# A relu² attention and a relu² feed-forward in one kernel: score visits of three tiles in spare PSUM banks, g sums ahead of squares, and one store per 128 tokens

## Chip, cores and metric

The kernel runs on one core of one Trainium2 chip. The metric is the device time of one execution in microseconds; the median over several executions is compared. The engines are named as the profile names them: PE is TensorE's matmuls, PEld its weight loads, DVE VectorE, ACT ScalarE, POOL GpSimd and SP SyncE.

## The reference, cut to what matters

Attention without softmax over 8 batches, 12 heads, 448 tokens and 64 elements per head, followed by a feed-forward layer from 768 to 2,048 and back.

```python
scores = matmul(q, k.transpose(0, 1, 3, 2)) / sqrt(64)
attn = maximum(scores, 0.0) ** 2 / 448
x = matmul(attn, v)                      # 8 x 12 x 448 x 64
x = x.transpose(0, 2, 1, 3).reshape(3584, 768)
h = x @ w_in                             # 3584 x 2048
g = maximum(h, 0.0) ** 2
out = g @ w_out                          # 3584 x 768, float32
```

## The kernel before, in words

**Tokens.** The 448 tokens of a batch are numbered `p * 7 + j`, with `p` from 0 to 63 and `j` from 0 to 6. A *row* of 128 output tokens is written `(pr, tb)`: pair of batches `pr` (0 to 3) and block `tb` (0 to 6). Its partitions 0 to 63 hold the tokens of one `j` and its partitions 64 to 127 those of the next. In six blocks of seven both `j` belong to one batch; in block 3 the second `j` is 0 of the pair's other batch.

**Attention.** A *unit* is four heads of one batch, three units to a batch, 24 in all. A unit has seven *score tiles*, one per `j`. `score(t)` computes one: four 64x64 matmuls of 448 columns that run side by side on the four quarters of the array, into a `slot` of two PSUM banks (two slots, `s_p`), and one ACT instruction (line 266) that takes the relu of 128x896 out of PSUM into an `at` tile. DVE squares it in place (line 369). When all seven tiles of a unit are there, `av_unit` multiplies them with v (28 matmuls, line 317), also into a slot, and ACT copies the result to `xt` (line 323).

**Feed-forward.** Batches 0 and 1 take w_in plainly (`h_group`, line 409). Batches 2 to 7 take it by a seven-product scheme with added and subtracted operands (`h_period`, line 538). w_out is always done in that scheme: `o_groups` makes of two rows a *group* of seven *products* k = 0 to 6, each of eight 128x128 matmuls of 384 columns (line 725). Pairs 0 and 2 have three groups and pairs 1 and 3 have four; I call these stages o0, o1, o2 and o3. Two accumulators hold a group: X takes products 0, 2, 4 and 5, Y takes 1, 3 and 6. They lie in bank pair `big[n % 2]` of two pairs (pools `mma` and `mmb`); the first product of group n + 1 is issued ahead of products 5 and 6 of group n and uses the other pair. What the text uses of a group:

- After k = 0 ACT copies X to `m1`; after k = 2 ACT copies X to `u2` (`end6`, line 627), and k = 4 then adds on to X; after k = 4 ACT copies X to `u3` (`end7`), and k = 5 adds on to X.
- After k = 1 (`end2`) the two output tiles `osb0` and `osb1` are taken anew (pool `osb`, two buffers for each) and DVE writes the first half of `osb0` (`plus`, line 632); k = 3 then overwrites Y.
- The left sides of products 2, 3, 4 and 6 are sums of g (`s1` to `s4`) that DVE makes in `sums` (line 594). `s3` is made after k = 2 and is used by k = 4.
- After k = 5 and k = 6 (`end4`, `end3`) the two rows are stored (`store`, line 561), each as two DMAs of 64 tokens. In the last group of all, `LAST`, the stores are made in halves and quarters of a row's width.

**Order.** Everything is written out in one order by the loop at the end of the kernel. It adds up the costs of the feed-forward's matmuls on a clock, and at certain matmuls (*edges*: first matmul of a w_in group, of most products of a w_in period, or of a w_out product) it calls what is due. A `visit` is a detour of PE from 128x128 to 64x64 matmuls: one score tile, `av_unit` if a unit is complete, then the other tiles. Visits of two tiles are spread evenly over the clock, with at least 1.5 us of it between two. DVE work that can wait is kept in the queues `due` (squares of score tiles) and `due_g` (squares of g) with due times, and `fill`, `flush` and `put` issue it. `prefetch` issues transposing DMAs on SP for later units and POOL issues the loads. SP issues the stores too.

Of the kernel before, what the change touches and what calls it, by code (L numbers as in the profile page):

```python
# [12 lines left out]
FP32 = mybir.dt.float32  # L13
AF = mybir.ActivationFunctionType
# [4 lines left out]
def kernel(  # L19
# [9 lines left out]
    nc = tc.nc  # L29

    B, H, S, D = q.shape
    NT, DM = out.shape
# [11 lines left out]
    J = 7  # L44
    PW = S // J
    NU = 3
    NUN = B * NU
# [7 lines left out]
    SK = 256.0  # L55
    CX = 1.0 / 896.0
# [137 lines left out]
    def slot(dtype, third=False):  # L194
        return (third_p if third else s_p).tile(
            [P, 2, 2048 // mybir.dt.size(dtype)], dtype, name="slot", tag="slot")
# [54 lines left out]
    now = [0]  # L251
    avt = [None]

    def score(t, times=1, third=False):
        n, j = divmod(t, J)
        qT, kT = qkt[n]
        ps = slot(FP32, third)
        for hh in list(range(2)) * times:
            r = slice(64 * hh, 64 * hh + 64)
            for hp in range(2):  # L260
                c = slice(64 * hp, 64 * hp + 64)
                nc.tensor.matmul(  # L262
                    ps[c, hh, 0:S], lhsT=kT[r, j, c], rhs=qT[r, :, c],
                    start=True, stop=True)
        at = at_p.tile([P, 2, S], FP16, name="at", tag="at")
        nc.scalar.activation(out=at, in_=ps[:, :, 0:S], func=AF.Relu, scale=SK)  # L266
        ats[t] = at
        seen[t] = now[0]

# [28 lines left out]

    unit = [NU]

    def av_unit():

        n = unit[0]
        if n == NUN or seen.get(n * J + J - 1, 10 ** 6) >= now[0]:
            return
        unit[0] += 1
        flush(rest=False)
        at_pe[0] += 1.33
        b, u = divmod(n, NU)
        vt = vts[n]  # L310
        ps = slot(FP32)
        for j in range(J):
            at = ats.pop(n * J + j)
            for hp in range(2):
                r = slice(64 * hp, 64 * hp + 64)
                for hh in range(2):
                    nc.tensor.matmul(  # L317
                        ps[64 * hh:64 * hh + 64, hp, 0:S],
                        lhsT=vt[r, hh, j * D:(j + 1) * D], rhs=at[r, hh, :],
                        start=(j == 0), stop=(j == J - 1))  # L320
        if u == 0:
            xts[b] = x_p.tile([P, NM, S], FP16, name="xt", tag="xt")
        nc.scalar.activation(
            out=xts[b][:, 2 * u:2 * u + 2, :], in_=ps[:, :, 0:S],
            func=AF.Copy, scale=CX)
# [16 lines left out]
    at_pe = [0.0]  # L342
    at_ve = [0.0]

    def flush(rest=True):
        for d in (due, due_g) if rest else (due,):
            while d:
                put(d)

    def put(d):  # L350
        ready, cost, fn, _ = d.popleft()
        at_ve[0] = max(at_ve[0], at_pe[0], ready) + cost
        fn()

    def fill(until):
        for d in (due, due_g):
            while d and max(at_ve[0], at_pe[0], d[0][0]) + d[0][1] <= until:
                put(d)
# [9 lines left out]
        due.append((at_pe[0] + lag, 0.54,  # L368
                    lambda: nc.vector.tensor_mul(at, at, at), 0))  # L369

    def visit(tiles):
        now[0] += 1
        for t in tiles:
            if t % J == 0 and t >= NPE * J:
                prefetch(t // J + 2)
        for t in tiles[:1]:
            score(t)
        av_unit()
        for t in tiles[1:]:
            score(t)  # L380
        at_pe[0] += 0.19 + 0.19 * len(tiles)
        for i, t in enumerate(tiles):
            square(ats[t], 0.6 + 0.85 * i)
# [5 lines left out]
    def mm_tile(i=None, dtype=FP32):  # L389
        if i is None:  # L390
            mm_no[0] += 1
            i = mm_no[0] % len(big)
        return big[i].tile(
            [P, 2048 // mybir.dt.size(dtype)], dtype, name="mm", tag="mm")
# [158 lines left out]
        return [(0.096, step(p, r, m), r == 0 and m == 0 and p not in (0, 1, 6, 8))  # L553
                for p in range(14) for r in range(2) for m in range(NH)]

    def store(row, osb, c, eng, eng2=None):
        pr, tb = row
        for i in range(2):
            b, j = divmod(2 * tb + i, J)
            b += 2 * pr  # L560
            (eng2 if eng2 and i else eng).dma_start(  # L561
                out=out[b * S:(b + 1) * S, :].rearrange(
                    "(p j) d -> p j d", j=J)[:, j, c],
                in_=osb[64 * i:64 * i + 64, c])
# [19 lines left out]
    def sums(i, rows, to):  # L584

        a1, a2 = tile_of(rows[0]), tile_of(rows[1])
        x, y = ((a2[:, LO], a2[:, HI]), (to.get(1), a1[:, LO]),
                (a1[:, LO], a2[:, LO]), (a1[:, HI], to.get(2)))[i - 1]
        to[i] = late["s"].tile([P, KH, P], FP16, name=f"s{i}", tag=f"s{i}")
        op = nc.vector.tensor_add if i == 1 else nc.vector.tensor_sub  # L590
        while due and due[0][0] <= max(at_ve[0], at_pe[0]) + 0.3:
            put(due)
        now_ve(0.6)
        op(to[i], x, y)  # L594

    def o_groups(groups, then):
# [5 lines left out]
        def group(n, rows, last):  # L602
# [3 lines left out]
            c0, c1 = slice(0, HALF), slice(HALF, DM)  # L606
# [63 lines left out]
            def end4():  # L670
                if last:
                    plus(1, c0, "u3", acc=Z)
                    store(rows[1], osb[1], c0, nc.gpsimd)
                    return
                nc.scalar.activation(out=osb[1][:, c0], in_=X[0][:, 0:HALF],
                                     func=AF.Copy, scale=CO)
                store(rows[1], osb[1], slice(0, DM), nc.sync)
                ahead(1, n + 1)
                ahead(2, n + 1)
# [5 lines left out]
            def end3_part(z):  # L685
                h = HALF // 2
                cc = slice(z * h, z * h + h)
                c = slice(HALF + cc.start, HALF + cc.stop)
                plus(0, c, "u5", acc=W, cc=cc)
                store(rows[0], osb[0], c, nc.sync, nc.scalar)  # L690

            products = (
                (X, True, lambda: tile_of(rows[0])[:, LO], b11, end1),
# [20 lines left out]
            def step(k, f):  # L714
                acc, fresh, left, right, end = products[k]
                if last and k == 5:
                    acc, fresh = Z, True

                def run():
                    if f == 0 and fresh and k != 3:  # L720
                        acc[:] = [mm_tile((n + (k == 5)) % 2)]
                    if f == 0 and k == 0:
                        ahead(1)
                        ahead(2)
                    nc.tensor.matmul(  # L725
                        acc[0][:, 0:HALF], lhsT=left()[:, f], rhs=right[:, f],
                        start=(fresh and f == 0),
                        stop=(f == KH - 1), skip_group_check=not fresh)
                    if f == KH - 1:
                        end()  # L730
                        if k < 4 and n + 1 < len(groups):
                            some = sum(d[3] <= needs(n + 1) for d in due_g)
                            for _ in range(-(-some // (4 - k))):
                                put(due_g)
                        fill(at_pe[0] + AFTER[k])
                return run

            ls = [[(0.1625, step(k, f), ((2 if k == 5 else True) if f == 0 else False))
                   for f in range(KH)] for k in range(7)]
            if last:  # L740
                ls[6] = [(0.0825, step3(z, f), False) for z in range(2) for f in range(KH)]
# [2 lines left out]
        def pre(i):  # L744
            sums(i, groups[0], sets[0])
# [30 lines left out]
    NB0 = NU * J  # L776
    ps = slot(FP32, True)
# [108 lines left out]
    events = []  # L886
    seq = [[2, 3], 4, [4, 5], [6, 7], [8, 9], 5, [10, 11], [12, 13], [14, 15],
           [16, 17], [18, 19], [20], []]
    for i, ts in enumerate(seq):
        at = (2.5 + i) * T_G  # L890
# [18 lines left out]
    for m in (6, 7):  # L909
        events.append((T_H + (1 + 3 * (m - 6)) * T_G, lambda m=m: prefetch(m)))  # L910
    at0 = T_H + 8 * T_G
    for pr in range(1, B // 2):
        t0 = 2 * NB0 * pr
        end = begin[pr] + T_S - 6.5
        gap = (end - at0) / 21
        for i in range(21):
            ts = [t0 + 2 * i, t0 + 2 * i + 1]
            events.append((at0 + i * gap, lambda ts=ts: visit(ts), True))
        at0 = end
        for i in range(4):  # L920
            events.append((begin[pr] - 6 + i, lambda b=2 * pr, i=i: sums_x(b, i)))
    events.append((at0 + 0.3, lambda: visit([]), True))

    def pre(pr, i):
        def run():
# [29 lines left out]
                steps += periods[b, i0]  # L955
        steps += outs[pr][0]

    clock, last = 0.0, 0.0
    ev = deque(sorted(events, key=lambda e: e[0]))
    for cost, fn, edge in steps:  # L960
        fired = 0
        while ev and edge and ev[0][0] <= clock + (1.6 if edge == 2 and not fired else 1e-3):
            if len(ev[0]) == 3:
                if clock < last + 1.5:
                    break
                last = clock
            ev.popleft()[1]()
            fired += 1
        if fn is not None:
            at_pe[0] += cost  # L970
            fn()
        clock += cost
# [31 lines left out]
```

## Time and profile before

| | |
|---|---|
| median of 8 executions | 370.81 us (370.6 to 371.39) |
| the profiled execution | 370.65 us; its span, first to last instruction, 368.9 us; granted TensorE clock 0.997 |
| PE busy | 359.5 us, 97% of the span, 3,588 matmuls |
| DVE, ACT, POOL busy | 265.2, 247.5 and 107.4 us |
| DMA issues of stores | 58 on SP, 2 on ACT, 2 on POOL |
| bytes moved | 42.64 MB |

"Busy" counts the time in which an engine has an instruction under way. Matmuls are pipelined, so PE busy includes the time it takes to change from one kind of matmul to another. In a timeline, `x8` behind a group of instructions is their number, and a time in square brackets is idle time ahead of it with what ended it. Times run from the span's start.

### The profile page before, as it was taken

What the parts mean: (1) busy time and instruction counts of PE and PEld (TensorE: products, weight loads), DVE (VectorE), ACT (ScalarE), POOL (GpSimd) and SP (SyncE); (2) the same over time, 40 slices, a digit from 0 to 9 for tenths busy, and PEclk for the clock granted to TensorE, in tenths of its full rate; (3) what the DMA queues carried; (4) which work ended last, traced back from release to release, by engine and by line L of the source; (5) the groups of instructions that cost most, each with busy time, mean ns of one, the idle gap of its engine ahead of it and who ended that gap; (6) DMA issues with size and microseconds to landing.
All of it is one profiled execution on the core that took longest, in us unless ns stands there. A gap on an engine that the chain in (4) does not pass through costs nothing.

```text
span 368.9 us, 8720 instructions
## 1 busy us (share of the span) xinstructions
PE 359.5 (97%) x3588; PEld 230.2 (62%) x3588; DVE 265.2 (72%) x470; ACT 247.5 (67%) x371; POOL 107.4 (29%) x128
## 2 busy tenths in 40 slices
PE   8899999999999999999999999999999999999994
PEld 3644445445555778875555588786555689976663
DVE  2997677997777787788585766989766686884442
ACT  3988894787676989876556588886765885532220
POOL 8545521846552255531225045140000000000001
PEclk9999999999999999999999999999999999999998
DMA  7999999999999999987699699591323300003333
GB/s 113 196 205 204 205 204 166 155 165 168 184 165 117 193 95 91 113 105 62 143 169 104 155 155 90 84 116 37 65 71 88 85 3 2 2 0 83 89 88 85
DMA packets 121159, 42.64 MB, mean 116 GB/s; under 512 B 100832, under 2 KB 117760, under 8 KB 121120
## 3 DMA queue, kind: packets, MB, share of 16 engines
q0 software_dynamic: 82912, 23.01, 63.2%
q1 hardware_dynamic: 38048, 18.98, 24.7%
q8 instruction: 28, 0.46, 0.5%
q10 hardware_dynamic: 160, 0.10, 0.1%
q14 instruction: 11, 0.09, 0.1%
HBM read 45.61 MB, written 11.01 MB: 154 GB/s over the span
## 4 chain that ended last, share of the span: by engine, by line
PE 90%; ACT 3%; DVE 3%; issue 2%; DMA 1%; POOL 0%; POOLq 0%; ACTq 0%
PE mm L725 34%; PE mm L538 27%; PE slot L262 10%; PE mm L409 9%; PE slot L317 7%; ACT at L266 3%; DMA k<-in_k_dram 1%; DVE at L297 1%; PE avt L280 1%; PE slot L238 1%; PE mm L238 0%; DVE at L369 0%; DVE xt L292 0%; ACT u L627 0%; DVE osb L632 0%
## 5 line engine op out<-in xcount | busy, mean ns | idle before, releaser
L266 ACT ACTIVATE at<-slot 128x896 f16<-128x896 f32 x168 | 145.8, 925 | 22.2 <-PE slot L262 22.2
L369 DVE TENSOR_TENSOR at<-at 128x896 f16<-128x896 f16 x147 | 87.1, 617 | 9.7 <-ACT at L266 9.6
L109 POOL DMA_DIRECT2D qs<-in_q_dram x36 | 35.3, 983 | 114.3 <-DMA qT<-qs 106.8
L725 PEld LDWEIGHTS <-s 128*128 128x128 f16 x440 | 41.5, 98 | 32.7 <-issue 3.6
L262 PE MATMUL slot<-qT,kT 64*64 64x448 f16 x744 | 56.8, 361 | 1.9 <-ACT at L266 1.4
L538 PEld LDWEIGHTS <-w 128*128 128x128 f16 x576 | 54.3, 98 | 5.1 <-issue 4.3
L538 PE MATMUL mm<-xt,w 128*128 128x224 f16 x432 | 48.9, 259 | 0.0
L725 PEld LDWEIGHTS <-g 128*128 128x128 f16 x336 | 31.7, 98 | 24.1 <-issue 4.7
L538 PEld LDWEIGHTS <-ws 128*128 128x128 f16 x432 | 40.3, 98 | 4.7 <-issue 4.7
L632 DVE SCALAR_TENSOR_TENSOR osb<-mm,u 128x384 f32<-128x384 f32 (+1 forms) x30 | 16.2, 542 | 36.5 <-ACT u L627 24.0
L725 PE MATMUL mm<-b,g 128*128 128x384 f16 x224 | 40.7, 326 | 0.0
L725 PE MATMUL mm<-b,s 128*128 128x384 f16 x216 | 39.6, 326 | 0.2 <-DVE s L594 0.2
L409 PE MATMUL mm<-xt,w 128*128 128x448 f16 x192 | 39.8, 354 | 0.0
L725 PE MATMUL mm<-t,s 128*128 128x384 f16 x224 | 39.3, 326 | 0.0
L109 POOL DMA_DIRECT2D ks<-in_k_dram x36 | 35.3, 983 | 8.6 <-DMA b<-in_moe_w_out_dram 5.8
L262 PEld LDWEIGHTS <-kT 64*64 64x64 f16 x744 | 19.0, 104 | 28.7 <-issue 23.3
L561 POOL DMA_DIRECT2D out_dram<-osb x2 | 1.1, 564 | 119.6 <-DVE osb L632 119.6
L627 ACT ACTIVATE u<-mm 128x384 f32<-128x384 f32 x28 | 13.7, 491 | 31.6 <-PE mm L725 27.1
L538 PE MATMUL mm<-x,ws 128*128 128x224 f16 x288 | 34.1, 259 | 0.0
L481 DVE CUSTOM_DVE_ANT_0 g<-mm,m 128x448 f16<-128x448 f32 x36 | 22.4, 622 | 15.2 <-PE mm L538 7.6
L317 PE MATMUL slot<-at,vt 64*64 64x448 f16 x588 | 31.9, 350 | 0.2 <-DVE at L369 0.2
L409 PEld LDWEIGHTS <-w 128*128 128x128 f16 x192 | 17.1, 98 | 19.2 <-issue 5.1
(76 smaller groups left out, 399.3 us busy)
## 6 DMA issues: line engine op xcount, KB each, us to landing
out_dram<-osb SPq DMA_DIRECT2D x52, 192.0 KB, 3.0
vt<-in_v_dram POOLq DMA_DIRECT2D x24, 224.0 KB, 6.3
qs<-in_q_dram POOLq DMA_DIRECT2D x36, 112.0 KB, 4.4
ks<-in_k_dram POOLq DMA_DIRECT2D x36, 112.0 KB, 4.8
w<-in_moe_w_in_dram POOLq DMA_DIRECT2D x8, 384.0 KB, 11.3
b<-in_moe_w_out_dram POOLq DMA_DIRECT2D x4, 768.0 KB, 17.1
q<-in_q_dram POOLq DMA_DIRECT2D x6, 224.0 KB, 7.7
k<-in_k_dram POOLq DMA_DIRECT2D x6, 224.0 KB, 8.4
```

Source lines behind the costliest of these rows:

```text
L109: nc.gpsimd.dma_start(out=t[:, :, hh, :], in_=heads(src, n)[:, hh].rearrange("p (j d) -> p j d", d=D))
L238: nc.tensor.transpose(pss[i][64 * hh:64 * hh + 64, i if n < 4 else 0, j * P:(j + 1) * P], src[:, hh, j * D:(j + 1) * D], ident)
L262: nc.tensor.matmul(ps[c, hh, 0:S], lhsT=kT[r, j, c], rhs=qT[r, :, c], start=True, stop=True)
L266: nc.scalar.activation(out=at, in_=ps[:, :, 0:S], func=AF.Relu, scale=SK)
L317: nc.tensor.matmul(ps[64 * hh:64 * hh + 64, hp, 0:S], lhsT=vt[r, hh, j * D:(j + 1) * D], rhs=at[r, hh, :], start=(j == 0), stop=(j == J - 1))
L369: lambda: nc.vector.tensor_mul(at, at, at), 0))
L409: nc.tensor.matmul(cell[0][:, 0:S], lhsT=w1[f // 4][:, m, (f % 4) * P:(f % 4 + 1) * P], rhs=xts[b][:, m, :], start=(m == 0), stop=(m == NM ...
L481: nc.vector._custom_dve(TENSOR_ADD_SAT, out=gs(s, hi, right), in0=acc(s, y), in1=keep[s, nm], s0=3.4e38, s1=0.0)
L538: nc.tensor.matmul(XY[s][y][:, r * Q:(r + 1) * Q], lhsT=left(k, i0 + 2 * s + r, m), rhs=right(k, m), start=(fresh and r == 0 and m == 0), ...
L627: nc.scalar.activation(out=t, in_=X[0][:, 0:HALF], func=AF.Copy, scale=CO)
L632: nc.vector.scalar_tensor_tensor(out=osb[row][:, c], in0=acc[0][:, 0:cc.stop - cc.start], scalar=CO, in1=keep[nm][:, cc], op0=ALU.mult, op ...
L725: nc.tensor.matmul(acc[0][:, 0:HALF], lhsT=left()[:, f], rhs=right[:, f], start=(fresh and f == 0), stop=(f == KH - 1), skip_group_check=n ...
```

## The change

1. In w_out groups the bank pair that group n does not use, number `(n + 1) % 2`, is lent to a visit at the edge of product 2 and, except in a stage's last group, at the edge of product 4. It is taken as two single-bank tiles, so what is evicted from it takes two ACT instructions of 128x448 in place of one of 128x896. Without attn x v in the visit the first score tile goes there, with it the attn x v. Such a visit has three tiles, but at product 4 two where attn x v is due.
2. The loop at the end no longer fires a list of even visits. It compares the number of tiles issued with a planned number. At the two edges named it visits where it is up to 1.5 tiles ahead of plan, and at other edges where it is not ahead (at product 5: up to 1.5 ahead), with two tiles.
3. `sums` no longer issues the due squares of which the clock says that they are ready; it issues those that end within 0.9 us of PE's clock (0.5 us for `s3`, less than the 0.54 us that a square counts).
4. A row whose 128 tokens are of one batch is stored by one DMA, whose target is written as 2 (`j`) x 64 (`p`) x columns and whose source is 128 partitions x columns. Block 3 keeps two DMAs. In the last group the stores go to SP, SP, ACT, ACT and SP, and none goes to POOL.

```diff
-    def score(t, times=1, third=False):
+    def score(t, times=1, third=False, ps=None):
...
+        spare = ps is not None
+        ps = slot(FP32, third) if ps is None else [mm_tile(ps), mm_tile(ps)]
...
-        nc.scalar.activation(out=at, in_=ps[:, :, 0:S], func=AF.Relu, scale=SK)
+        if spare:
+            for hh in range(2):
+                nc.scalar.activation(
+                    out=at[:, hh], in_=ps[hh][:, 0:S], func=AF.Relu, scale=SK)
+        else:
+            nc.scalar.activation(out=at, in_=ps[:, :, 0:S], func=AF.Relu, scale=SK)
...
+    def av_due(more=0):
         n = unit[0]
-        if n == NUN or seen.get(n * J + J - 1, 10 ** 6) >= now[0]:
+        return n < NUN and seen.get(n * J + J - 1, 10 ** 6) < now[0] + more
...
-    def visit(tiles):
+    def visit(tiles, spare=None):
...
-            score(t)
-        av_unit()
+            score(t, ps=None if av_due() else spare)
+        av_unit(spare)
...
-    def store(row, osb, c, eng, eng2=None):
+    def store(row, osb, c, eng):
+
         pr, tb = row
+        b, j = divmod(2 * tb, J)
+        if j + 1 < J:
+            b += 2 * pr
+            eng.dma_start(
+                out=out[b * S:(b + 1) * S, :].rearrange(
+                    "(p j) d -> j p d", j=J)[j:j + 2, :, c],
+                in_=osb[:, c])
+            return
         for i in range(2):
             b, j = divmod(2 * tb + i, J)
             b += 2 * pr
-            (eng2 if eng2 and i else eng).dma_start(
+            eng.dma_start(
...
-        while due and due[0][0] <= max(at_ve[0], at_pe[0]) + 0.3:
-            put(due)
+
+        fill(at_pe[0] + (0.5 if i == 3 else 0.9))
         now_ve(0.6)
...
-                    store(rows[1], osb[1], c0, nc.gpsimd)
+                    store(rows[1], osb[1], c0, nc.scalar)
...
-                store(rows[0], osb[0], c, nc.sync, nc.scalar)
+                store(rows[0], osb[0], c, (nc.scalar, nc.sync)[z])
...
-            ls = [[(0.1625, step(k, f), ((2 if k == 5 else True) if f == 0 else False))
+            free = (n + 1) % 2
+            edges = {2: (free, 3, 3)} if n == len(groups) - 1 else {
+                2: (free, 3, 3), 4: (free, 3, 2)}
+            ls = [[(0.1625, step(k, f),
+                    ((edges.get(k), k == 5) if f == 0 else False))
                    for f in range(KH)] for k in range(7)]
...
+        if edge and clock >= plan[0][0]:
+            pair, soon = edge if edge is not True else (None, False)
+            ahead = tile_no - planned(clock)
+            if tile_no == NT:
+                if unit[0] < NUN and clock > last + 1.5:
+                    visit([])
+                    last = clock
+            elif pair is not None and ahead <= 1.5 and clock > last + 1.25:
+                n = min(pair[1 + av_due(1)], NT - tile_no)
+                visit(list(range(tile_no, tile_no + n)), pair[0] if n == 3 else None)
+                tile_no += n
+                last = clock
+            elif ahead <= (1.5 if soon else 0.0) and clock > last + 1.5:
+                n = min(2, NT - tile_no)
+                visit(list(range(tile_no, tile_no + n)))
+                tile_no += n
+                last = clock
```

More of the change, by code (lines that the diff above doesn't have):

```diff
@@ L252 @@
     avt = [None]
-    def score(t, times=1, third=False):
+    def score(t, times=1, third=False, ps=None):
         n, j = divmod(t, J)
         qT, kT = qkt[n]
-        ps = slot(FP32, third)
+        spare = ps is not None
+        ps = slot(FP32, third) if ps is None else [mm_tile(ps), mm_tile(ps)]
         for hh in list(range(2)) * times:
@@ L262, in score @@
                 nc.tensor.matmul(
-                    ps[c, hh, 0:S], lhsT=kT[r, j, c], rhs=qT[r, :, c],
+                    ps[hh][c, 0:S] if spare else ps[c, hh, 0:S],
+                    lhsT=kT[r, j, c], rhs=qT[r, :, c],
                     start=True, stop=True)
         at = at_p.tile([P, 2, S], FP16, name="at", tag="at")
-        nc.scalar.activation(out=at, in_=ps[:, :, 0:S], func=AF.Relu, scale=SK)
+        if spare:
[4 more added lines that the diff above has]
+            nc.scalar.activation(out=at, in_=ps[:, :, 0:S], func=AF.Relu, scale=SK)
         ats[t] = at
@@ L299, with av_unit @@
     unit = [NU]
-    def av_unit():
+    def av_due(more=0):
         n = unit[0]
-        if n == NUN or seen.get(n * J + J - 1, 10 ** 6) >= now[0]:
+        return n < NUN and seen.get(n * J + J - 1, 10 ** 6) < now[0] + more
+    def av_unit(ps=None):
+        if not av_due():
             return
+        n = unit[0]
         unit[0] += 1
@@ L310, in av_unit @@
         vt = vts[n]
-        ps = slot(FP32)
+        spare = ps is not None
+        ps = [mm_tile(ps), mm_tile(ps)] if spare else slot(FP32)
         for j in range(J):
@@ L317, in av_unit @@
                     nc.tensor.matmul(
-                        ps[64 * hh:64 * hh + 64, hp, 0:S],
+                        ps[hp][64 * hh:64 * hh + 64, 0:S] if spare
+                        else ps[64 * hh:64 * hh + 64, hp, 0:S],
                         lhsT=vt[r, hh, j * D:(j + 1) * D], rhs=at[r, hh, :],
@@ L322, in av_unit @@
             xts[b] = x_p.tile([P, NM, S], FP16, name="xt", tag="xt")
+        if spare:
+            for hp in range(2):
+                nc.scalar.activation(
+                    out=xts[b][:, 2 * u + hp], in_=ps[hp][:, 0:S],
+                    func=AF.Copy, scale=CX)
+            return
         nc.scalar.activation(
@@ L554, in h_period @@
                 for p in range(14) for r in range(2) for m in range(NH)]
-    def store(row, osb, c, eng, eng2=None):
+    def store(row, osb, c, eng):
         pr, tb = row
+        b, j = divmod(2 * tb, J)
[5 more added lines that the diff above has]
+                in_=osb[:, c])
+            return
         for i in range(2):
@@ L911 @@
     at0 = T_H + 8 * T_G
+    plan: list = []
     for pr in range(1, B // 2):
@@ L914 @@
         end = begin[pr] + T_S - 6.5
[L915 to L918, printed above, removed]
+        plan.append((at0, end, t0))
         at0 = end
@@ L921 @@
             events.append((begin[pr] - 6 + i, lambda b=2 * pr, i=i: sums_x(b, i)))
-    events.append((at0 + 0.3, lambda: visit([]), True))
     def pre(pr, i):
@@ L956, with planned @@
         steps += outs[pr][0]
-    clock, last = 0.0, 0.0
+    def planned(t):
+        n = 0.0
+        for a, e, t0 in plan:
+            if t >= a:
+                n = t0 + min(1.0, (t - a) / (e - a)) * 2 * NB0
+        return n
+    clock, last, tile_no = 0.0, 0.0, 2 * NB0
+    NT = NUN * J
     ev = deque(sorted(events, key=lambda e: e[0]))
     for cost, fn, edge in steps:
[L961 to L965, printed above, removed]
-                last = clock
-            ev.popleft()[1]()
-            fired += 1
+        while ev and edge and ev[0][0] <= clock + 1e-3:
+            ev.popleft()[1]()
+        if edge and clock >= plan[0][0]:
[9 more added lines that the diff above has]
+                tile_no += n
+                last = clock
+            elif ahead <= (1.5 if soon else 0.0) and clock > last + 1.5:
[3 more added lines that the diff above has]
+                last = clock
         if fn is not None:
```

## The prediction, made before the changed kernel had run

> **What bounds the kernel now.** I read the page first: shares of busy time, then the chain that ended last.
>
> ```profile
> PE 359.5 (97%) x3588; PEld 230.2 (62%) x3588; DVE 265.2 (72%) x470; ACT 247.5 (67%) x371; POOL 107.4 (29%) x128
> ...
> PE 90%; ACT 3%; DVE 3%; issue 2%; DMA 1%; POOL 0%; POOLq 0%; ACTq 0%
> ```
>
> PE sets the end almost everywhere, so a change pays only by what it takes from PE's row or puts in front of it. Next the timeline of PE in one w_out stage.
>
> ```profile
> 105.33 1.48 PE L725 MATMUL mm<-b,s 128*128 128x384 f16 x8
> 106.64 1.46 PE L725 MATMUL mm<-b,g 128*128 128x384 f16 x8
> 108.03 0.57 PE L262 MATMUL slot<-qT,kT 64*64 64x448 f16 x8
> 108.54 1.64 PE L725 MATMUL mm<-t,s 128*128 128x384 f16 x9
> ```
>
> A product takes 106.64 - 105.33 = 1.31 us. From 106.64 to 108.54 is 1.90, so a visit of two tiles costs 0.60. The 28 matmuls of attn x v (seven rounds of four) take 1.33 a unit, 0.19 a round, and a tile is one round. So 0.60 - 2 x 0.19 = **0.22 us is fixed in each visit**; nearly all visits of this trace repeat it within 0.01. Then where PE waits in spite of this, on all engines:
>
> ```profile
> 203.86 0.49 ACT L627 ACTIVATE u<-mm 128x384 f32<-128x384 f32 x1
> 203.99 0.62 DVE L369 TENSOR_TENSOR at<-at 128x896 f16<-128x896 f16 x1 [0.18 <-ACT at L266]
> 204.53 0.68 DVE L594 TENSOR_TENSOR s<-g 128x1024 f16<-128x1024 f16 x1
> ...
> 205.27 0.50 PE L725 MATMUL mm<-b,s 128*128 128x384 f16 x2 [0.20 <-DVE s L594]
> ```
>
> `s3` stands behind two squares and holds product 4 for 0.36 us against the usual pitch. At 113.7 an attn x v waits 0.47 for its last square. These two and some 0.3 us in w_in visits are all that PE loses to waits after 66 us. Last, the stores: their issues in the view of the tile `osb` (ns of an issue, first and last), the write of `osb0` that starts a group's output in the timeline, and a stretch of the windows view (busy time of the five engines, clock, DMA share, GB/s):
>
> ```profile
> L561 SPq DMA_DIRECT2D out_dram<-osb x58: 466/581/737, 93.2 to 364.2; - x58
> ```
>
> ```profile
> 348.30 0.56 DVE L632 SCALAR_TENSOR_TENSOR osb<-mm,m 128x384 f32<-128x384 f32 x1 [0.80 <-PE mm L725]
> ```
>
> ```profile
> 338.00:342.00 4.00, 4.00 (x26) 2.41 (x25) 2.15 (x4) 0.49 (x1) 0.00 (x0) 1.00 0.72 197
> ```
>
> Four DMAs of 64 rows x 3,072 bytes go out in a burst and use 0.72 of all 16 DMA engines: 197 / (16 x 0.72) = 17.1 GB/s for a busy engine, 180 ns for a row of 3,072 bytes. In the trace's packets of that stretch a row takes 121 ns where fewer engines write at once, 180 to 250 in the thick of it; a row of 1,536 bytes takes 62, one of 768 takes 36. From a store's issue to its first packet are 1.1 us, from its last packet to the landing 0.6.
>
> [...] the trace has 552 and 925, and starts 0.44 (113.83 to 114.27) and 0.81 us apart. [...] a DMA runs on k of the 16 engines[...] Stores of 64 rows on both sides get 16, and the share above agrees. [...]
>
> **Part 1 and 2: visits.** I walked the final loop's clock with the costs of the listing. It gives 64 visits after the first pair's before, and 58 after: 4, 11, 13, 11, 11, 10, 4 in h, o0, w_in, o1, w_in, o2, w_in become 4, 10, 12, 9, 11, 7, 5. Thirteen have three tiles. Gain: 6 x 0.22 = **1.3 us** on PE's path; rounds of matmuls stay as they are.
>
> What the third tile costs is ACT's. A spare tile adds 2 x 0.552 - 0.925 = 0.18 us of ACT, and the visit puts three evictions in its queue. With the visit's first matmul at 0, evictions start at 0.43, 0.87, 1.31 and 2.13, and `u2`, queued behind them, runs from 2.92 to 3.41. Product 4 adds on to the X that `u2` reads. It could start at 0.50 + 0.19 + 2 x 1.305 = 3.30, and starts at 3.47 (0.06 from the end to PE): 0.17 lost. The same holds for `u3` and product 5. A visit between them covers it. By the walk eight places have no such visit (product 4 in the last group of o0, in groups 0, 2, 3 of o1 and 1, 2 of o2; product 5 after o1's group 1 and o2's group 0): 8 x 0.17 = **1.4 us** lost. The spare banks themselves are free in time: the last DVE read, `end3`, ended at 107.40 and the visit came at 108.03.
>
> **Part 3: sums first.** The 0.36 at 205 goes (product 4 there is among the eight). The wait at 113.7 goes too: its tile now has two further products' time. With w_in's visits moved, I take 0.9 us gained. Squares come later by a sum, 0.68; an attn x v needs its last square only in its seventh round, 1.14 us in, so I take nothing, up to 0.5 lost. Parts 1 to 3: -1.3 + 1.4 - 0.9 = **-0.8 us**.
>
> **Part 4: the store.** It removes 27 of 62 issues. SP waits, none of them is on PE's path: nothing gained but some 0.1 us at the end. POOL's two last issues go to ACT, which has nothing else to do then. What counts is how long one takes. Its target is 2 x 64 rows, its source 128[...]: 64 x 0.121 = 7.7 us (I take the row of the quiet stretches, since two writers are fewer than 16) where four rows an engine, twice, took about 1 us. It is bounded by 64 x 0.18 = 11.5 from above[...]. All the stores of this form share those two engines.
>
> A group makes two such stores, 15.5 us of the two engines. In o3, where nothing else runs, a group lasts seven products, 9.1 us. **The bound moves from PE to two DMA engines.** `end2` of group n + 2 takes the buffer `osb0` of group n, and DVE's `plus` waits there for the landing; behind it in DVE's queue stand sums and squares, and product 3, which overwrites Y, waits for it. In the times of before, for o3:
>
> - Group 0: issued at 337.1 and 338.4; packets 338.2 to 345.9 and to 353.7; landed 354.3. `plus` of group 2, at 348.30 now, ends at 354.9, and product 3 starts 5.6 us late.
> - Group 1: on to 361.4 and 369.2; landed 369.8. `plus` of group 3 would be at 363.0; product 3 loses 6.4 more.
> - Group 2: 7.7 and, for block 3 with its two old DMAs, 1.0: to 378.0.
> - Group 3: three halves of 64 x 0.062 = 4.0 and two quarters of 64 x 0.036 = 2.3: 16.6, to 394.6, landed 395.2, where the last one lands at 367.3 now. [...]
>
> That is **+27.9 us** in o3. Where visits stretch the groups to some 12 us the backlog is smaller. o0: the row that group 2 needs is done at 110.5, or 114.6 if one 32 ns load packet goes between two rows (the loads are dense there); product 3 would start at 109.8: 1.3 to 5.4 lost, I take 3.3. o1 likewise: 1.9 in group 2 and 3.3 in group 3, 5.2, up to 8 with loads. o2: 0 to 3, 0.5. Transposes on SP's queue land some 15 us later, but are issued two units ahead: nothing, up to 5. Sum: 27.9 + 3.3 + 5.2 + 0.5 = **+36.9**.
>
> Total -0.8 + 36.9 = +36.1. On the profiled execution's 370.65, which is 0.16 below the median, and on the median alike: **406.9 us** from 370.81.
>
> **Rivals.**
>
> - *The store spreads over all 16 engines.* Its place is the issue of each store, its price 128/k rows one after another, and it decides from k: at 16 a store takes 1 us and hides under any group, as now; at 8 only the last one shows, by about 1 us; at 4, with 3.9, the last group's backlog does. Then -0.8 and -0.1 at the end: 369.9, faster. For it: today's stores do so, and both forms write the same rows. [...]
> - *Sixteen engines, and ACT holds the products longer.* Three evictions at full length without overlap (0.55, 0.55, 0.92, 0.92) make it 0.6 in place of 0.17 a place: 8 x 0.43 = +3.4, 373.3, slower. The starts 0.44 and 0.81 apart speak against it. Without any hold it would be 368.5.
> - *Two engines, but rows at 180 ns.* o3 alone then needs the two engines until about 421; with the earlier stages some 440.
> - *The change doesn't do what it says:* fewer than six visits saved. That is worth 1.3 us at most, and lost among the others.
>
> **Numbers.** k = 2 has 0.85: 406.9, with 389 (rows a seventh faster, nothing lost before o3) to 432 (three quarters of the way to the slow rows) holding all but 0.05. Sixteen engines with the short hold have 0.11 (369.9), with a long one 0.04. Below 370.07, over 0.2% faster, which is about what a measurement of this kernel can tell from no change: 0.08; within: 0.05; slower: 0.87. The range 389 to 432 holds 0.8; the other sign is outside.
>
> **What would show it.** Right: a DMA wait on `plus` line 632 (osb) in groups 2 and 3 of o3, 6 to 7 us each; store landings of 8 us and more in place of 3.0; about 85 GB/s falling below 55 in o3; PE idle there; 13 pairs of 128x448 relu evictions. Wrong: stores that land in 3 to 4 us with the DMA share spread as now; then the three-tile visits decide, by PE's delay at product 4 behind `u2`.

## The result, and the profile after

The changed kernel takes **439.7 us** (median of 11 executions, 435.9 to 441.3) against 370.7 (median of 30): ratio 1.184, interval 1.182 to 1.186. The forecast was 406.9 and its range ended at 432. The side and the main mechanism were right, half of the size was missing. The profiled execution took 440.04 us; its span is 438.3, which is 69.4 more than before. All traces are compared by their spans.

The page of the kernel after, engines first, then the chain that ended last by engine and by line:

```profile
PE 373.2 (85%) x3588; PEld 237.8 (54%) x3588; DVE 264.8 (60%) x470; ACT 249.3 (57%) x384; POOL 105.0 (24%) x126
...
PEclk9999999999899967999996999789999999996785
...
PE 58%; DMA 27%; DVE 5%; issue 3%; ACT 2%; SPq 0%; DVEq 0%; ACTq 0%
PE mm L559 21%; DMA out_dram<-osb 21%; PE mm L755 15%; PE mm L430 8%; PE slot L263 6%; DMA kT<-ks 5%; PE slot L329 5%; ACT at L273 2%; DVE at L388 2%; DVE osb L662 1%; PE slot L200 1%; DVE at L304 1%; DVE s L624 1%; PE avt L287 1%; SPq L120 0%
```

PE had 97% and falls to 85%. Of the chain, DMA had 1% and now holds 27%, in two items: the stores (21%) and, not forecast, a transpose of k (5%). PE is also *busier* by 13.7 us with the same 3,588 matmuls: they got slower. The clock's row shows where, in dips to 6, 7 and 5 that were not there before.

What the engines waited for (us in total, times, longest):

```profile
DVE osb L662 <- DMA out_dram<-osb: 36.7, 6, 9.6
...
PE mm L755 <- DVE osb L662: 25.1, 6, 7.4
...
PE slot L263 <- DMA kT<-ks: 12.1, 1, 12.1
```

The first two are the chain that the forecast drew: `plus` waits for the landing of `osb0`'s store, and product 3 waits for `plus`. One of them, group 2 of o3, in the timeline, and the stretch of that stage's store traffic in the windows view (five engines, clock, DMA share, GB/s):

```profile
396.96 0.56 DVE L662 SCALAR_TENSOR_TENSOR osb<-mm,m 128x384 f32<-128x384 f32 x1 [7.60 <-DMA out_dram<-osb]
397.43 0.68 DVE L624 TENSOR_TENSOR s<-g 128x1024 f16<-128x1024 f16 x1
397.57 1.76 PE L755 MATMUL mm<-t,s 128*128 128x384 f16 x5 [6.21 <-DVE osb L662]
```

```profile
384.00:388.00 4.00, 4.00 (x27) 2.40 (x25) 1.85 (x3) 1.47 (x3) 0.00 (x0) 1.00 0.13 52
```

A DMA share of 0.13 is two engines of sixteen, where the burst of before had 0.72; from 379 to 388 two packets of the stores are under way for 7.6 us and three for 0.4. The trace's packets of 3,072 bytes have a median of 121 ns.

Where the 69.4 us are, from PE's timeline against that of before:

| | forecast | measured |
|---|---|---|
| parts 1 to 3 | -0.8 | -1.2 |
| product 3 behind `osb0`: o0, o1, o2 | 3.3, 5.2, 0.5 | 4.8, 10.2, 0.7 |
| a score tile in w_in behind a late transpose of k | 0, up to 5 | 12.1 |
| PE in w_in, waiting for nothing that the profile shows | none | 6.3 |
| PE at half clock after four of these waits | none | 7.9 |
| o3 and the end | 27.9 | 27.5 |
| small, not assigned | | 1.1 |

### The profile page after: what moved, and what is told of

Read it like the earlier page. It is cut to its first block, busy times and chain, and to the rows that moved or that the text cites. A ratio compares the mean times of both kernels' runs of the same rounds, so it can differ in the third digit from the quotient of the medians.

```text
span 438.3 us, 8701 instructions
## 1 busy us (share of the span) xinstructions
PE 373.2 (85%) x3588; PEld 237.8 (54%) x3588; DVE 264.8 (60%) x470; ACT 249.3 (57%) x384; POOL 105.0 (24%) x126
## 4 chain that ended last, share of the span: by engine, by line
PE 58%; DMA 27%; DVE 5%; issue 3%; ACT 2%; SPq 0%; DVEq 0%; ACTq 0%
PE mm L559 21%; DMA out_dram<-osb 21%; PE mm L755 15%; PE mm L430 8%; PE slot L263 6%; DMA kT<-ks 5%; PE slot L329 5%; ACT at L273 2%; DVE at L388 2%; DVE osb L662 1%; PE slot L200 1%; DVE at L304 1%; DVE s L624 1%; PE avt L287 1%; SPq L120 0%
## 5 line engine op out<-in xcount | busy, mean ns | idle before, releaser
L273 ACT ACTIVATE at<-slot 128x896 f16<-128x896 f32 x156 | 135.6, 927 | 25.7 <-PE slot L263 25.7
L388 DVE TENSOR_TENSOR at<-at 128x896 f16<-128x896 f16 x147 | 86.1, 617 | 10.5 <-ACT at L273 10.1
L755 PEld LDWEIGHTS <-s 128*128 128x128 f16 x440 | 44.3, 103 | 62.7 <-issue 38.1
L109 POOL DMA_DIRECT2D qs<-in_q_dram x36 | 35.1, 978 | 158.5 <-DMA qT<-qs 150.5
L263 PE MATMUL slot<-qT,kT 64*64 64x448 f16 x696 | 54.3, 362 | 20.4 <-DMA kT<-ks 12.1
L755 PE MATMUL mm<-t,s 128*128 128x384 f16 x224 | 44.8, 354 | 25.1 <-DVE osb L662 25.1
L559 PEld LDWEIGHTS <-w 128*128 128x128 f16 x576 | 55.4, 101 | 8.2 <-issue 6.4
L559 PE MATMUL mm<-xt,w 128*128 128x224 f16 x432 | 51.5, 267 | 0.0
L755 PE MATMUL mm<-b,s 128*128 128x384 f16 x216 | 42.4, 342 | 0.0
L559 PE MATMUL mm<-x,ws 128*128 128x224 f16 x288 | 35.9, 269 | 0.5 <-issue 0.5
L662 DVE SCALAR_TENSOR_TENSOR osb<-mm,m 128x384 f32<-128x384 f32 x14 | 7.8, 556 | 43.6 <-DMA out_dram<-osb 36.7
L508 DVE TENSOR_TENSOR g<-g 128x896 f16<-128x896 f16 x48 | 28.6, 616 | 0.4 <-ACT g L511 0.4
```

The lines of the kernel that those rows point to most:

```text
L109: nc.gpsimd.dma_start(out=t[:, :, hh, :], in_=heads(src, n)[:, hh].rearrange("p (j d) -> p j d", d=D))
L263: nc.tensor.matmul(ps[hh][c, 0:S] if spare else ps[c, hh, 0:S], lhsT=kT[r, j, c], rhs=qT[r, :, c], start=True, stop=True)
L508: lambda: nc.vector.tensor_mul(g, g, g), b))
L559: nc.tensor.matmul(XY[s][y][:, r * Q:(r + 1) * Q], lhsT=left(k, i0 + 2 * s + r, m), rhs=right(k, m), start=(fresh and r == 0 and m == 0), ...
L662: nc.vector.scalar_tensor_tensor(out=osb[row][:, c], in0=acc[0][:, 0:cc.stop - cc.start], scalar=CO, in1=keep[nm][:, cc], op0=ALU.mult, op ...
L755: nc.tensor.matmul(acc[0][:, 0:HALF], lhsT=left()[:, f], rhs=right[:, f], start=(fresh and f == 0), stop=(f == KH - 1), skip_group_check=n ...
```

## Experiments

My theory, A: the new store runs on two engines (the share of 0.13 above), and this alone makes the loss, by three ways: `osb0`'s landing, transposes behind the stores in SP's ring (the queue of DMAs that one issuing engine feeds, q1 on the page for SP and q10 for ACT), and PE's clock after a long wait. Rivals: the number or form of the DMAs matters rather than k, the number of engines; something else of the change costs time before o3; the slow matmuls come from traffic and not from waiting.

**1. All but the store** (`e1_old_store`). The old `store` and its old queues put back into the changed kernel.

> The changed kernel with the old store (two DMAs of 64 rows, the old queues): parts 1 to 3 alone. Theory (the store's two DMA engines cost everything): 369.9 us, between 369.3 and 370.6, ratio to before 0.997; 58 visits, thirteen of three tiles, product 4 held by about 0.15 us behind the u2 copy in eight places. Rival (the three-tile visits hold ACT and PE): 400 us or more, near the changed kernel's 440.

Measured: 369.56 us, ratio 0.9967 [0.9954, 0.9979], so faster than both kernels. Parts 1 to 3 give -1.26, and the store the rest: +70.2.

**2. The store alone** (`e2_only_store`), in the kernel before.

> The kernel before with part 4 alone, the new store and its queues. Theory: as slow as the changed kernel, 430 to 450 us; stores land in 8 us and more, DVE waits for osb, transposes land late, PE at half clock after each long wait. Rival (visits are the cause): 371.

Measured: 436.4 us, ratio 1.1757 [1.1707, 1.1807]. Its waits:

```profile
DVE osb L641 <- DMA out_dram<-osb: 32.4, 6, 7.6
...
PE mm L734 <- DVE osb L641: 22.7, 6, 6.2
```

The visits are not needed for the loss.

**3. 62 + 2 rows, or 60 + 4, in the old form** (`e3_62_2`, `e4_60_4`). In the kernel before each DMA of 64 tokens is cut in two. My assumption was that a DMA of 62 rows runs on two engines, as the new store does, and one of 60 on many more:

```diff
+            for lo, hi in ((0, 62), (62, 64)):        # e4: (0, 60), (60, 64)
                 (eng2 if eng2 and i else eng).dma_start(
-                    out=...[:, j, c], in_=osb[64 * i:64 * i + 64, c])
+                    out=...[lo:hi, j, c], in_=osb[64 * i + lo:64 * i + hi, c])
```

> The kernel before; each DMA of 64 rows is cut into one of 62 and one of 2 rows. Same form of target (one run of rows), twice the issues. Theory[...]: 425 to 450 us. Rival (the two-dimensional target or the single long DMA is slow in itself): 371 to 373.

> The kernel before; each DMA of 64 rows is cut into one of 60 and one of 4 rows: the control of the cut into 62 and 2, with the same number of issues. Theory: [...] 370.5 to 372.5 us. Rival (more and smaller DMAs are the cost): as slow as the cut into 62 and 2.

Measured: 445.75 us (1.2024 [1.2007, 1.2041]) for 62 + 2, and 373.22 (1.0071 [1.0057, 1.0084]) for 60 + 4. The waits of the former:

```profile
DVE osb L633 <- DMA out_dram<-osb: 35.6, 6, 8.0
...
PE slot L262 <- DMA kT<-ks: 13.2, 1, 13.2
```

Both have the same number of DMAs and neither has the new target. 60 + 4 costs 2.4 us, and in its trace there is no such wait of DVE or PE. 62 + 2 costs 74.9 and has the waits of the changed kernel: 35.6 us for `osb` where that has 36.7, and 13.2 for `kT` where that has 12.1. So neither twice as many issues nor the new form of the target is what costs; the count of rows in a DMA decides. That this works by the number of engines is what A says, and the waits agree; on how many engines the 62 rows and the 60 ran was not shown.

**4. The new store in o3 alone** (`f1_o3_only`).

```diff
-        if j + 1 < J:
+        if j + 1 < J and pr == 3:
```

> The changed kernel with the new store in the last w_out stage o3 alone (and for the one row of pair 2 that is written there in the old form, with two DMAs); stages o0, o1 and o2 store with two DMAs of 64 rows as before. Theory A (what is lost ahead of o3 comes from the stores of o0 and o1 alone: their landings, the transposes behind them and PE's slow clock after each wait): the time ahead of o3 returns to that of parts 1 to 3 alone, and o3 adds its 27.5: 369.6 + 27.5 = 397, within 3. Theory B (the 27.5 in o3 contains a backlog carried over from earlier stages): o3 adds well under 27, below 392. Theory C (something else of the change costs time ahead of o3): above 402.

Measured: 394.56 us, ratio 1.0642 [1.0623, 1.0661]. Up to the first product of o3 its PE is within 0.2 us of `e1_old_store`. So nothing but the stores of o0 to o2 costs time before o3: rival C falls. o3 adds 24.4 by the spans, against 27.5. Row (2, 6), which is stored in o3 but belongs to pair 2, goes out in the old form here, which had the share of 0.72 before, and `osb0` is late once, by 7.7 us, not twice. The time lies inside A's margin of 3 us and above B's 392: nearly all of o3's loss needs no backlog from earlier stages.

**5. Transposes out of the stores' ring** (`f4_act_ring`): ACT issues the stores of o0 to o2.

```diff
+        if pr < 3:
+            eng = nc.scalar
```

> The changed kernel with the stores of o0, o1 and o2 issued by ACT in place of SP, so that the transposing DMAs of q and k, which SP issues, no longer stand behind them in SP's ring; the stores still use the same form, and ACT now waits for DVE's write ahead of each issue. Theory A (the transposes of k land late because they queue behind the slow stores in one ring): the waits of PE for kT of 12.3 us after o0 and of about 6.5 after o1 go, with the two slow restarts of about 2 us each: 440 - 19 - 4 = 417, up to 427 if ACT's own waits for DVE cost some of it. Theory B (they land late because the two engines that carry the stores also carry an eighth of each transpose, whichever ring it came by): the waits stay, 435 to 442. The waits of DVE for osb stay in both.

Measured: ratio 1.1625 [1.1553, 1.1697], which of 370.87 is 431.1 us; the trace is of an execution of 435.1. PE has no wait for `kT` left, where the changed kernel has 12.1. What took its place:

```profile
DVE osb L664 <- DMA out_dram<-osb: 38.7, 5, 13.2
...
ACT at L270 <- issue: 12.2, 2, 6.6
...
PE mm L559 <- issue: 5.7, 2, 3.7
```

PE's wait for k is gone, as A said and B did not. But A's reason holds only in part, as SP's issues of q's transposes show (ns, shortest, median and longest; the changed kernel, then this one):

```profile
L120 SPq DMA_TRANSPOSE qT<-qs x18: 1221/1281/15734, 60.0 to 302.3; - x18
```

```profile
L120 SPq DMA_TRANSPOSE qT<-qs x18: 1222/1227/4527, 60.1 to 292.7; - x18
```

Behind stores in its own ring SP is held in one issue for up to 15.7 us, and k's transpose, which is issued after q's, goes out that much later; without them for 4.5 us at most (8.2 for one of k). The transposes themselves are no faster. From issue to landing the three of k behind o0's stores take 24.2, 14.3 and 20.0 us here, against 10.6, 13.5 and 10.1 in the changed kernel and 3.0, 4.1 and 3.9 in the kernel before. So they are slow in a ring without stores too, and B's cause, the two shared engines, is not excluded: in the kernel before, a transpose of k issued at 263.7 has 13 to 21 packets under way for 1.9 of its 2.7 us, where a new store has two. B's eighth is my estimate, two engines of sixteen. No run separates this cause from others.

The gain is some 9 us and not 13 to 23. ACT is now held by its own DMA issues (up to 4.0 us for one, where 0.5 is usual), and PE has two waits in w_in, 5.7 us together, that end on nothing that the profile shows. The expectation had also put the changed kernel's 6.3 us after o1 down to `kT`; its chain of waits gives it to nothing either:

```profile
276.42 0.30 PE slot L263
276.72 6.27 issue
283.00 0.96 PE slot L263 x7
```

The trace has hints. The wait falls between two matmuls of one score tile, where no semaphore is waited for. Packets of 16 KB in the queue that the page calls "instruction" come 10 to 16 us apart at that point of the kernel before. In the changed kernel one starts at 256.6 and the next at 280.5; that one ends at 281.4, and PE goes on at 283.0. `e2_only_store` and `f7_o3_pool` (experiment 6) have the same wait, 6.2 and 5.3 us long, and PE goes on 1.7 and 1.6 us after the end of such a packet. With the stores on ACT such packets end at 141.6 and 157.7, and PE goes on at 145.0 and 159.2. So the wait may have to do with these packets. No run here tests that; it stays open.

**6. Another choice of engines in o3** (`f7_o3_pool`): POOL issues the stores of o3.

```diff
+        if pr == 3 or row == (2, 6):
+            eng = nc.gpsimd
```

> The changed kernel with the stores of o3 (and the one row of pair 2 stored there) issued by POOL in place of SP and ACT, in the same form with 2 as its slowest dimension. Theory A[...]: a single store still takes some 8 us but several run side by side, the buffer of group n is free before group n + 2 wants it, and o3's 27.5 shrink to the last store's own length, 4 to 8 us: 440 - 20 to 440 - 23.5, 416 to 420. Theory B (POOL's stores take the same two engines, or one store at a time by itself is the cost): 436 to 442. [...]

Measured: ratio 1.1358 [1.1321, 1.1395]; the profiled execution took 422.37, and o3 adds 14 in place of 27.5. The windows view of two stretches:

```profile
381.00:384.00 3.00, 3.00 (x21) 1.79 (x19) 1.85 (x3) 0.98 (x2) 0.18 (x1) 1.00 0.25 98
404.00:406.00 2.00, 2.00 (x14) 1.20 (x13) 0.00 (x0) 0.36 (x1) 0.00 (x0) 1.00 0.71 141
```

With two stores in flight the share is 0.25, four engines. In the changed kernel it was 0.13 from 384 to 388, with stores issued at 378.9 and 380.3 on SP; in its last group, where SP and ACT both issue, two packets of 1,536 bytes are under way for 9.9 of 12.5 us and never more than three. So the new stores run side by side from POOL where SP's and ACT's stand in line. Why they do was not shown. The 0.71 does not tell for the new form alone: the two DMAs of block 3, in the old form, are issued at 401.6 and 402.2. One store by itself is no faster: the first five take 11 to 16 us from issue to landing. That, and one more wait of DVE for `osb0`, 6.0 us, keeps o3's part from falling to the 4 to 8 expected.

**7. Sums first alone, and visits alone** (`f5_sums_only`, `f6_visits_only`). The former is the kernel before with this line in `sums`, the latter `e1_old_store` with it undone:

```diff
-        while due and due[0][0] <= max(at_ve[0], at_pe[0]) + 0.3:
-            put(due)
+        fill(at_pe[0] + (0.5 if i == 3 else 0.9))
```

> The kernel before with part 3 alone: sums ahead of squares, even visits of two tiles and old stores. The prediction's step says -0.9: some 370.0 against 370.8. If only the delay of 0.36 us at one product 4 goes and later squares hold an attn x v instead, it is -0.4 to +0.1.

> Parts 1 and 2 alone: the changed kernel with the old stores and with the old order of sums and squares. The prediction's steps say 6 fewer visits x 0.22 = -1.3 and up to 8 holds x 0.17 = +1.4, so 370.8 to 370.9, no change. The holds in the changed kernel's trace were four of 0.15, which makes it -0.7: 370.1. If the old order of sums is what the three-tile visits can't stand (squares ahead of s3 hold product 4), it is 371 or more and part 3 owns the whole gain of 1.2.

Measured: 370.38 us (0.9992 [0.9984, 1.0001]) for sums alone, and **375.67** (1.0138 [1.0124, 1.0152]) for visits alone; both together gave 369.56. So sums are worth 0.3 in the kernel before and 6.1 beside three-tile visits. The timeline of the visits alone shows why:

```profile
109.47 2.28 DVE L388 TENSOR_TENSOR at<-at 128x896 f16<-128x896 f16 x4
...
111.94 0.62 DVE L388 TENSOR_TENSOR at<-at 128x896 f16<-128x896 f16 x1 [0.18 <-ACT at L273]
112.48 0.68 DVE L616 TENSOR_TENSOR s<-g 128x1024 f16<-128x1024 f16 x1
...
113.23 0.99 PE L747 MATMUL mm<-b,s 128*128 128x384 f16 x5 [0.87 <-DVE s L616]
```

Five squares stand ahead of `s3`, and product 4 waits for it: 1.03 us against the usual pitch, at six places. Where sums go first, `s3` runs at 110.44 and product 4 starts 0.15 late, behind `u2`.

**8. A wait of PE by itself** (`g5_pe_wait`, `g10_pe_wait`): `e1_old_store` in which DVE writes the first half of `osb0` 5 or 10 times more. In the first, A is that a wait as short as this leaves the clock alone.

```diff
                 new_osb()
+                for _ in range(5 if (pr, n) == (3, 2) else 0):     # or 10
+                    plus(0, c0, "m1")
                 plus(0, c0, "m1")
```

> The version with the old stores (369.6), in which DVE writes the first half of osb0 six times in place of once in group 2 of o3 alone: the five extra writes hold product 3 by about 2.0 us (five of some 0.5 less 0.5 that were free) without any DMA in it. Theory A[...]: the 2.0 and nothing more, 371.5 to 371.8, and matmuls at full pitch after it. Theory B (any wait costs a slow restart): 373.2.

> The same with ten extra writes: product 3 waits about 4.5 us. Theory A (a long wait lets TensorE's clock fall to a half and costs another 1.6 us or more, whatever it was that PE waited for): 369.6 + 4.5 + 1.6 to 2.2 = 375.7 to 376.3, with 384-column matmuls at 0.31 in place of 0.16 us for some 3 to 4 us. Theory B (the slow matmuls after the waits of the changed kernel come from the stores' traffic, or from the operands' arrival, and not from the wait): 374.1, full pitch.

The condition on `pr` held in all four stages and not in o3 alone, since `pr` there is the program's outer variable, so each kernel has four waits and the expected totals don't apply. Measured: 377.85 us (1.0193 [1.0173, 1.0213]) and 401.01 (1.0824 [1.0807, 1.0841]). What decides is in the traces. With five, PE loses 1.67, 1.73, 1.67 and 2.52 us at product 3, and every matmul after it has its full pitch. With ten it loses 4.63, 4.69, 4.63 and 5.49, and then 10 to 17 matmuls start 0.320 us apart in place of 0.163. One stage of each, the windows of 1 us after the wait, PE first and the clock third from the end:

```profile
113.00:114.00 1.00, 1.00 (x8) 0.61 (x7) 1.00 (x4) 0.00 (x0) 0.00 (x0) 1.00 1.75 138
```

```profile
376.00:377.00 1.00, 1.00 (x4) 0.47 (x4) 1.00 (x2) 0.00 (x0) 0.00 (x0) 0.50 0.02 8
377.00:378.00 1.00, 1.00 (x5) 0.44 (x3) 0.07 (x1) 0.00 (x0) 0.00 (x0) 0.50 0.00 0
```

The clock is 1.00 after the shorter wait and 0.50 after the longer one, and in the second stretch no DMA runs to speak of. So a wait is enough, without stores of the new form. The slow matmuls cost 1.5 to 2.6 us beside the wait itself.

## Why the prediction was right or wrong

**Parts 1 to 3: sum right, one term wrong.** 58 visits after the first pair's, thirteen of three tiles: as walked. The hold behind `u2` and `u3` is 0.146 us at eight places in `e1_old_store`, 1.2 in all; it was put at 1.4. The term for sums, -0.9, was sized as if it stood alone. Alone it is -0.3. Its real work is to prevent the 1.03 us that three-tile visits would lose at six places. The forecast counted what the third tile does to ACT's queue and not what it does to DVE's, where its square is one more ahead of `s3`. Nor does the wait at 113.7, which the forecast counted here, go with sums alone: that attn x v still loses 0.47 there; it goes where visits move too.

**Part 4, k = 2: right,** though that the new store would run on two engines was my assumption; no trace of before shows such a store. The changed kernel's has the share of 0.13. The rival of sixteen engines, 369.9, was about what the version without the new store gave, 369.56. That neither the number of the DMAs nor the new target is what costs is shown by 62 + 2 against 60 + 4.

**o3: right,** 27.9 against 27.5, since there the sum is 64 rows by 121 ns on two engines that nothing else uses much. From o3's first store to the last landing the forecast has 58.1 us (337.1 to 395.2), and so has the trace (378.9 to 437.0). The clock, which the forecast left out, costs PE 4.8 us in o3 too, but there the two engines set the end: PE is done at 420.9. One reading was a little low: 62 ns is the shortest row of 1,536 bytes in the trace of before, the median is 65, worth 0.6 us over three half stores.

**o0 to o2: mechanism right, row too cheap.** 9.0 forecast, 15.7 measured. o0's 4.8 lies within its 1.3 to 5.4, o1's 10.2 above its "up to 8". The step that failed is 7.7 us for a store. In o1 the two stores of group 1, issued at 212.7 and 213.4, kept the two engines until about 232.4: 18.7 us for 128 rows, 146 ns a row in place of 121, or 9.3 us a store, beside the loads. The wait of group 3 was 7.6 in place of 3.3.

**The transposes: the largest miss.** "Nothing, up to 5" became 12.1 us, at 151.8. The step that failed is the delay, "some 15 us later". The cover was there: in the kernel before, this unit's transpose of k landed at 130.2, 16.4 us ahead of PE's first use. In the changed kernel it landed at 164.2, 34 us later, where PE itself came 5.6 us later. The chain of waits of the kernel after, then SP's issues from the timeline:

```profile
125.90 13.53 DMA kT<-ks
...
152.24 1.82 SPq L120
...
154.16 10.07 DMA kT<-ks
164.23 0.04 issue
164.27 0.59 PE slot L263 x4
```

```profile
138.32 15.73 SPq L120 DMA_TRANSPOSE qT<-qs  x1
154.16 3.45 SPq L120 DMA_TRANSPOSE kT<-ks  x1
```

A transpose had a median of 4.0 us from issue to landing before; these two took 13.5 and 10.1. That is the smaller part. SP, which had just issued two stores, was held for 15.7 us in the issue of q's transpose, where 1.7 was the longest before, and so issued k's only after PE had come to its tile. "Issued two units ahead" is no fixed lead either: a transpose that lands late frees its `qs` or `ks` buffer late, and POOL then loads late (its waits for `qT` went from 106.8 to 150.5 us). The forecast took SP's waits to be off PE's path; this one was on it.

With the stores on ACT, SP issued this transpose at 137.5 and PE did not wait. It landed at 157.5 all the same, and PE, held up elsewhere, came to the tile at 162.5 only; at 152.2, as in the changed kernel, it would have waited some 5 us by my estimate. So the held issue is shown as one cause, and what makes the landing itself slow is open. The 6.3 us after o1 are another wait, and open too.

**The clock: missing.** In the changed kernel each wait of over 4 us is followed by 9 to 27 matmuls at half clock, 1.3 to 2.9 us. Before o3 that is four times, 7.9 us. The prediction listed each wait at its bare length. Waits that cost PE 2.59 us and less leave the clock at 1.00 in the changed kernel and in experiment 8, and those of 4.05 and more bring it to 0.50. In `e2_only_store` a shorter one than these was enough (a loss of 2.66 us; PE's timeline, then a window after it, the clock again third from the end):

```profile
212.42 0.80 PE L734 MATMUL mm<-t,s 128*128 128x384 f16 x2 [2.50 <-DVE osb L641]
```

```profile
213.00:214.00 1.00, 1.00 (x5) 0.46 (x4) 1.00 (x3) 0.00 (x0) 0.81 (x1) 0.50 0.12 49
```

Together: 6.7 for the rows, 12.1 and 6.3 in w_in and 7.9 for the clock are 33.0. By the spans the change costs 69.4 where 36.1 was forecast, 33.3 more.

## What to carry to other kernels

Before two DMAs are made one, write down the outermost count of each side. Here a target of 2 x 64 rows in place of 64 turned stores of 1.6 us (the packets of two take 3.3 us at 338 in the kernel before) into stores of 7.5 to 9.3, and those of SP and ACT stood in line, two packets at a time. A slow DMA costs three times over: its own buffer, whatever the same engine has to issue behind it, and PE's clock after a wait. Here every wait of 4.05 us and more that I read, and one of 2.66, had the half clock behind it, and those of 2.59 and less had not. So add about 2 us to each long wait of PE; the slow matmuls cost 1.3 to 2.9 us here. And two parts of a change may be one: a bigger visit without sums first loses 5 us, with it the pair gains 1.3; test them apart and together.

## What the runs showed of the hardware that I had not expected

- A store on two engines moves 128 rows of 3,072 bytes, half on each, at 121 ns a row where little else runs, and at 146 beside loads.
- Stores of the same form from POOL run side by side: a DMA share of 0.25 in place of 0.13 with two in flight, at 11 to 16 us a store.
- With stores of two engines queued, the issue itself blocks: ACT was held up to 4.0 us by one issue of a store, and SP up to 4.3, where 0.5 was usual; SP's issue of a transpose behind such stores took up to 15.7 us, where 1.2 was usual.
- Transposes were slow beside such stores from another ring too: with the stores on ACT they took 12.5 to 24.2 us from issue to landing at k of six units, where 4.0 was the median before.
- PE's waits of 1.67 to 2.59 us left the granted clock at 1.00 in the changed kernel and in `g5_pe_wait`; one of 2.66 us in `e2_only_store` and those of 4.05 to 12.1 us in the changed kernel brought it to 0.50 for some 3 to 6 us of work.
